# First scan of a fused state-space and two-FFN kernel: split loads, alternating PSUM tiles, new issue order

## The chip, the cores and the metric

The kernel runs on one core of a Trainium2 chip. The metric is the device time of one execution in microseconds (us); the time of a version is the median of its runs.

## What is computed

The inputs are `x` (4 batches, 8 heads, 768 steps, 32 values), a decay `a` per step, and `B`, `C` with 16 states per step. A causal scan with decay runs over the 768 steps, and two feed-forward networks follow on the 3072 rows of 256 values that it gives:

```
log_a = log(clip(a, 1e-6, 1))
per chunk:  cum = cumsum(log_a);  L = exp(cum_i - cum_j) for i >= j, else 0
            y   = ((C B^T) * L) x  +  (C state) * exp(cum)
            state = exp(sum log_a) * state + sum_j B_j x_j exp(cum_end - cum_j)
h = x @ w_in;   g = h if h > 0 else exp(h) - 1;   x2 = g @ w_out
out = ((x2 @ w1) * (x2 @ w2) @ w3) @ w_out2
```

All data are float32. Where precision matters the kernel splits a matrix into a high part, rounded to the matmul format, and a low part, the rest, and replaces one product by three matmuls (`mm3`, lines 394 to 397).

## The kernel before, in words

**Chunks and tiles.** A chunk is 128 rows of one position in the sequence (two blocks of 64 steps) for all batches and heads; there are 24 chunks of data, and four chunks make one tile of 512 rows. The first four chunks, 0 to 3, are the *first scan*. Their path is separate from that of the later ones because their L comes from the decays by TensorE, not through a store and reload in DRAM.

**One chunk of the first scan**, as steps with the letters that name them in the order string:

- `0`, `9`, `4` (`first_parts`, L430): all decays are clipped on VectorE, the first column of each block is set to zero, and the high and low parts `hl` are made.
- `A` (`at_wide`, L493): two matmuls spread the decays of the chunk over 128 partitions (8 rows by 512 columns) into a PSUM tile. I call them A0 to A3.
- `l` (`at_prep`, L504): a VectorE scan of 512 columns turns that into L, in SBUF (scan0 to scan3). It needs the constant `eye`, made in `constants`. `5` (`at_bd`, L514) is GpSimd's product of B with the last column of L.
- `U` (`first_cb`, `cb_products` L524): the products C B of a pair of chunks (CB01, CB23), 32 small matmul records a pair, from the columns `bt` and `cz` of the chunk's load. `D` (`decayed`, L539): L = CB * L on VectorE (D0 to D3).
- `J` (`first_u`): the products B x of a pair (U01, U23). `6` copies them to SBUF on ScalarE (st), `?` and `8` finish the states on GpSimd; `C` (`at_cd`, L543) decays C there, after `7` (`at_decay`, four VectorE instructions from L473).
- `Q` (`first_y`, `y_products` L595): the outputs of a pair, first the products with L (L603), then those with the states (L609), which need `?` and `C` (Y01, Y23). `z` and `Y` split them into `xTh` (ScalarE) and `xTl` (VectorE), the input of the first network.

**PSUM.** The four tiles of the first scan, `f0`, `f1`, `f2` and `acc_f`, are `[128, 2, 512]`, two banks each, and are shared: A0 and A1 go into the two halves of `f2`, A2 and A3 into `acc_f`; the CB of chunks 0 and 2 share `f0`, those of 1 and 3 share `f1`; U and the outputs of both pairs share `f2` and `acc_f`. The first three are the three buffers of the pool that later holds the products of the first network (`h`), so its first three tiles take their places.

**The first network.** `v` (`half_a`, L712) computes half a unit, 12 matmuls of 256 columns, on the outputs of chunks 0 and 1 alone; v0 and v1 are the first halves of units 0 and 1. `a` (`unit_a`, L717) is the rest (a0, a1: 12 of 256 columns; later units 12 of 512), `x r s` its gate, `b` (`unit_b`, L749) the second product. The first four `b` are plain float32 products, 8 matmul records of 512 columns. From the fifth gate on the high part is made by `h`, the low part by `i` (VectorE) or `T` (GpSimd), as `POOL_LO` says.

**Weights** come as pieces of 512 KB, loaded by SyncE's queue (SP) in the order of `PIECES` (`wi0` to `wi7`, `wo0` to `wo7` and so on), three ahead of the order string, the rest by `N`. A piece is prepared by `k` (shift; on ScalarE or VectorE by `SCALAR_LOW`), `j` (scale, ScalarE), `K` (join, VectorE), `H` (high part, ScalarE) and `I` (low part; GpSimd for `wi0`, VectorE for the others here).

**Loads of a chunk.** `at_load` (L444) loads one block of 896 columns, 448 KB, into `xbc`. The later chunks' L come by two DMAs of 128 KB each (`M`, L490), their `xbc` by `X`.

**What sets the order.** `ORDER` is a string of letters, and each letter issues the next waiting step of its kind. `in_order` (L657) chains the instructions of every engine, the DMA queues among them, in the order in which the string issues them. So an instruction that waits holds back all that stand behind it on its engine. In the kernel before, `at_first`, `constants` and the first loads stand outside `in_order`, and the framework places them.

The first steps by engine, before:

```
PE   A0 A1 A2 A3 CB01 CB23 U01 Y01 U23 Y23 v0 a0 v1 a1 a2 b0 a3 b1 CB45,U45 a4 b2 a5 Y45 b3
DVE  clip memset lo(hl) scan0 scan1 scan2 decay D0 scan3 D1 join(wi0) D2 join(wi1) xTl0 xTl0' shift(wi2) D3
SP   a, xbc0, xbc1, pr, xbc2, xbc3, wi0, wi1, wi2, store, wi3, wi4, wo0, wo1, wi5, wo2, L4, pr1, wi6, L5, xbc4, wo3, xbc5
```

Of the kernel before, what the change touches and what calls it, by code (L numbers as in the profile page):

```python
# [22 lines left out]
DM = NH * D
# [11 lines left out]


ORDER = """
094AAlAl5Al5U7UJD6lk?C6j?!DNCkKC5jD5QHN8JKzIzY66NYHk?jD8kNK?jCI8QkNvK8zzYHYNkjaIHKjvMIHkxIaPkrKaNkxsjMLrbKjXxsNrkKaRHXBj
WMIjCbsxNrLXKBWsujNkaKDHMDtbxLNjIBr?tXK?jaCskCkKNhLxiyBrCbMKzsHNjkzYWkuXHYKaIHDjNtWI?bDxXKrtPI?jsHMykIazjXYKzhYNLahiBxMT
LrbXxsrBNVuHshMbRjiCaCDtt?aDxIrVNkhKbVxijrsaSLhsTaxkjLSrb?xsrkVHsyhIbPzzYBiXCBaKNYHKhkXRuxTbrMtHtMIsbhDCNDj??kiIhKyaLjNk  # L40
zBzYHKbMIKHxYILNHarCjsIMaihCBNxkkriaXjsxXbxNrrswjLhKBaLHkIijfbNsxK1FHbrIhsNkuSSwDhijtK?bHfIjFDkaNKhtHi?BxCIyrbPzszkXKjaY
hXiTYNuxbrMDKsMbthD?kCjktaiRaxCr?swxLrLhBbHsfIHFINyazBzYTXhYKMaixrNsbxMkrLXjswBhKjikufKHLbHItF?NtCaDh?KB1IDaxTNrjsbxrsSy
SazMYkzkMYhwPjiKaHxIHCNrbIxsXrKwfshNFTufXjbktDHkFItHDahKILCwLBxTrsa?R?axCrfsbjHKIFhByHibMIzxYMrbXhszYuLaDBtt?i?wDxLafNhr
iXbFxs1NbhBCrijskyKjbkhzzY3YKu%&aSt&D3tDC&a=Th=S=xa?&?x=TNrbrsCxsbhNjirkhsyTbzKjkYKaz%&=bxh^&ira&=&=sbx=rYNhsaih3iaxNjr3
bksxrbks@jKhKa&Th=&a@=%x#rbxsrTsaS&S=&#bx=^Nh^@ia@1r#h3#^asNjxirkbK@sxrkb#@sh#jia3hKi%&b&x=31@=r#a^&sh=&ib/x=rsbh/i|ch_b
i/|m_b/GSg]e|[EncS{(1m_)|}G>3e]_g.<cn,*[(mE}G.{e],<)nE>g*{.c[,dm*(.G}.)*]e.>gn<E.,*(.{c[})m,<g,G[e,.d>nd,]c.,(m,*d}E$*e.
{G.,)*]<d.>dng$,*.E+[c{.d,md,.g$,([,d@}G@#<d]#3d@)*+e>En#^d.{(+c*@})@d#m^e.,dnG,@*g.>(]#^c[}Eme.{G@,)n<.d,<$g>]d,[(*.#cd
m,3.g}.d,E#*G{3d,^e.+)n,d]*(.>E[+*c}dm+d.<2g{e,<)n+G.,(.*d>]}c.,d[,Eme,.d{*G+nd],2*d.+E.,d*.d<)2{d>3g,*d[+c.,2(m).}G.,<g
]>e[,En,d.{c*,(m)$*}d.>g.,G*.d,]e.,d.,cn<E[d*{$(+$)m}d@,<d.>G@#e]g#.c,nE@,*[d{m(+^.G}d,e*@+d])#.*En>d.{g^#([).,^d@}c@,em
d,.g#@G,[d<nd#*](>E}<.c{em#.G,n)],*d>g+E*.d{.(,*.d}[d+c.<)m+e*.>g2nG+[<(,]d,c}Emd.{d.,G$,),e>*gn+d[<2c*.,dm(],*G.}d.,E]*  # L50
.d+.e{2g,<nE[).{d,(,d}d>),.c>$*dm,eg*.dn,G[*c.+d.<2dm+.(,$G]g$}E.d{]d,[<e,dn).+d.,E>d,c,(m+d.G,d]}${e<E.dn{(,d}<)g>).d.,
[,d>.d,dd+++++
"""
# [39 lines left out]
X_RAW = {0: "s0 0", 4: "s0 1", 2: "s1 0", 5: "s1 1", 1: "s2 0"}  # L93
P_RAW = {0: "l0 0", 4: "l0 1", 2: "l1 0", 5: "l1 1", 1: "s2 1"}, {0: "h0 0", 4: "h0 1", 2: "l2 0", 5: "l2 1", 1: "i7 1"}

XCOLS = (("x", DM), ("bn", NH * N), ("bt", 2 * R), ("cz", 2 * 2 * R), ("cp", SUB * R))
XC = sum(n for _, n in XCOLS)

@with_exitstack
def kernel(  # L100
# [358 lines left out]

# [575 lines left out]
    at_first()
    constants()
    for k in range(2):
        at_load(k)
    at_pr(0)
    for k in range(2, CPT):  # L1040
        at_load(k)
    for p in queue[:3]:
        p.load()
# [72 lines left out]
```

## Time and profile before

| | us |
|---|---|
| median of 3 runs | 520.39 (519.7 to 520.78) |
| the profiled execution, its own time | 519.32 |
| its span, first to last instruction | 517.6 |
| TensorE (PE) busy | 504.3 (97%) |
| VectorE (DVE) busy | 406.6 (79%) |
| ScalarE (ACT) busy | 338.1 (65%) |
| GpSimd (POOL) busy | 242.0 (47%) |

Busy times are sums over the span; 1.7 us of the execution's own time lie outside it. In the rows below, times are from the span's start. A timeline row has start, length, engine, line of the kernel, operation, the tile written and the tiles read, and in square brackets how long the engine sat idle before it and what ended that. Instructions of one engine overlap a little, so what a sequence costs is the distance of the starts, not the sum of the lengths.

### The profile page before, as it was taken

What the parts mean: (1) busy time and instruction counts of PE and PEld (TensorE: products, weight loads), DVE (VectorE), ACT (ScalarE), POOL (GpSimd) and SP (SyncE); (2) the same over time, 40 slices, a digit from 0 to 9 for tenths busy, and PEclk for the clock granted to TensorE, in tenths of its full rate; (3) what the DMA queues carried; (4) which work ended last, traced back from release to release, by engine and by line L of the source; (5) the groups of instructions that cost most, each with busy time, mean ns of one, the idle gap of its engine ahead of it and who ended that gap; (6) DMA issues with size and microseconds to landing.
All of it is one profiled execution on the core that took longest, in us unless ns stands there. A gap on an engine that the chain in (4) does not pass through costs nothing.

```text
span 517.6 us, 9978 instructions
## 1 busy us (share of the span) xinstructions
PE 504.3 (97%) x3978; PEld 408.4 (79%) x3978; DVE 406.6 (79%) x548; ACT 338.1 (65%) x511; POOL 242.0 (47%) x224
## 2 busy tenths in 40 slices
PE   5799999999999999999999999999999999999996
PEld 3675678788878888888788888888887888878885
DVE  5888899996657655657687669957899898988874
ACT  2786777677665666653675888766765668566631
POOL 2612252572342452641445173977487555655410
PEclk9999999999999999999999999999999999999999
DMA  8994680564360734213321223010001110001002
GB/s 293 314 286 132 214 238 20 146 180 146 123 211 5 192 125 135 80 39 95 146 82 32 91 88 128 9 63 0 1 22 41 60 43 1 1 22 41 20 1 81
DMA packets 28174, 51.04 MB, mean 99 GB/s; under 512 B 2304, under 2 KB 10880, under 8 KB 28128
## 3 DMA queue, kind: packets, MB, share of 16 engines
q1 hardware_dynamic: 27984, 50.28, 31.3%
q8 instruction: 31, 0.51, 0.4%
q10 hardware_dynamic: 144, 0.13, 0.1%
q14 instruction: 15, 0.12, 0.1%
HBM read 44.01 MB, written 6.39 MB: 97 GB/s over the span
## 4 chain that ended last, share of the span: by engine, by line
PE 95%; POOL 2%; DMA 1%; DVE 1%; SPq 0%; issue 0%; DVEq 0%; ACT 0%; POOLq 0%
PE acc L395 10%; PE acc L396 9%; PE acc L397 9%; PE h L395 9%; PE h L396 9%; PE h L397 9%; PE p L395 4%; PE p L397 4%; PE p L396 4%; PE acc L757 3%; PE p_E L395 2%; PE p_E L397 2%; PE p_E L396 2%; PE p_d L397 2%; PE p_d L396 2%; PE p_d L395 2%
## 5 line engine op out<-in xcount | busy, mean ns | idle before, releaser
L733 DVE SCALAR_TENSOR_TENSOR e<-e,h 128x1024 f32<-128x1024 f32 x44 | 53.4, 1214 | 37.3 <-ACT e L728 33.3
L726 ACT ACTIVATE e<-h 128x1024 f32<-128x1024 f32 x48 | 49.3, 1027 | 50.0 <-PE h L397 47.6
L395 PE MATMUL h<-xTh,w_in 128*128 128x512 f32 (+1 forms) x200 | 78.8, 394 | 0.4 <-DVE g L733 0.4
L396 PE MATMUL h<-xTl,w_in 128*128 128x512 f32 (+1 forms) x200 | 76.9, 384 | 0.0
L397 PE MATMUL h<-xTh,w_in 128*128 128x512 f32 (+1 forms) x200 | 76.7, 383 | 0.0
L395 PE MATMUL acc<-g,w_out 128*128 128x512 f32 x176 | 69.7, 396 | 0.0
L396 PE MATMUL acc<-g,w_out 128*128 128x512 f32 x176 | 68.6, 390 | 0.0
L397 PE MATMUL acc<-g,w_out 128*128 128x512 f32 x176 | 68.5, 389 | 0.0
L738 ACT CAST g<-e 128x1024 fp32r<-128x1024 f32 x44 | 46.1, 1050 | 17.9 <-PE acc L397 15.1
L171 DVE TENSOR_TENSOR g<-e,g 128x1024 fp32r<-128x1024 f32 x31 | 42.1, 1357 | 15.0 <-ACT g L738 14.9
L171 POOL TENSOR_TENSOR g<-e,g 128x1024 fp32r<-128x1024 f32 x13 | 32.6, 2506 | 41.5 <-ACT g L738 34.9
L728 ACT ACTIVATE e<-e 128x1024 f32<-128x1024 f32 x48 | 50.7, 1060 | 1.0
L517 POOL TENSOR_TENSOR xbc<-xbc,L 128x128 f32<-128x128 f32 x24 | 16.1, 673 | 69.0 <-DVE L L511 32.6
L395 PEld LDWEIGHTS h<-xTh,w_in 128*128 128x128 f32 x200 | 38.3, 191 | 8.4 <-DVE g L733 0.5
L397 PEld LDWEIGHTS h<-xTh,w_in 128*128 128x128 f32 x200 | 38.2, 191 | 7.3
L396 PEld LDWEIGHTS h<-xTl,w_in 128*128 128x128 f32 x200 | 38.3, 192 | 7.1 <-issue 0.5
L395 PEld LDWEIGHTS acc<-g,w_out 128*128 128x128 f32 x176 | 33.0, 188 | 7.3
L397 PEld LDWEIGHTS acc<-g,w_out 128*128 128x128 f32 x176 | 33.0, 188 | 7.0
L396 PEld LDWEIGHTS acc<-g,w_out 128*128 128x128 f32 x176 | 33.1, 188 | 6.4
L171 POOL TENSOR_TENSOR w<-raw_wc,w 128x512 fp32r<-128x512 f32 x16 | 22.5, 1410 | 25.6 <-ACT w L249 12.3
L911 POOL TENSOR_TENSOR room_l<-room_l,room_o 128x512 f32<-128x512 f32 x12 | 19.0, 1582 | 26.6 <-DVE room_o L908 18.2
L511 DVE TENSOR_TENSOR_SCAN L<-L,eye 128x512 f32<-128x512 f32 x20 | 25.8, 1298 | 0.1
(438 smaller groups left out, 1318.4 us busy)
## 6 DMA issues: line engine op xcount, KB each, us to landing
xbc<-in_xc SPq DMA_DIRECT2D x24, 448.0 KB, 6.3
raw_wc<-in_w3t SPq DMA_DIRECT2D x16, 512.0 KB, 5.9
L<-a_cut SPq DMA_DIRECT2D x40, 128.0 KB, 5.8
raw_wi<-in_w_in SPq DMA_DIRECT2D x8, 512.0 KB, 8.7
raw_wo<-in_w_out SPq DMA_DIRECT2D x8, 512.0 KB, 7.5
x_dram<-x SPq DMA_DIRECT2D x6, 512.0 KB, 4.0
room_s<-x_dram SPq DMA_DIRECT2D x12, 256.0 KB, 3.7
out_t<-out SPq DMA_DIRECT2D x11, 256.0 KB, 2.0
```

The costliest lines, as they stand in the source:

```text
L171: eng.tensor_tensor(out=lo, in0=raw, in1=hi.bitcast(F32), op=ALU.subtract)
L395: T.matmul(out, wlo, xhi, start=first, stop=False, **kw)
L396: T.matmul(out, whi, xlo, start=False, stop=False, **kw)
L397: T.matmul(out, whi, xhi, start=False, stop=last, **kw)
L511: V.tensor_tensor_scan(out=flat, data0=wide, data1=eye.rearrange("p h s -> p (h s)"), initial=0.0, op0=ALU.mult, op1=ALU.add)
L517: G.tensor_tensor(out=c["bd"], in0=c["bn"], in1=c["L"][:, :, R - 1:R].to_broadcast([P, NH, N]), op=ALU.mult)
L726: A.activation(e, h, AF.Exp)
L728: A.activation(e, e, AF.Relu, scale=-1.0, bias=1.0)
L733: V.scalar_tensor_tensor(out=gt[t, n] if plain else e, in0=e, scalar=-1.0, in1=h, op0=ALU.mult, op1=ALU.max)
L738: A.copy(hi, e)
L757: T.matmul(acc, word_of(n)[:, j, es], g[:, j], start=m == 0, stop=False)
L911: GATE[m % 2].tensor_tensor(out=s["two"], in0=s["two"], in1=s["u2"], op=ALU.mult)
```

## The change

It has four parts.

1. **Constants and decays.** The high part of `hl` is made by VectorE, not ScalarE; the copy that makes `eye` moves behind the low part of `hl`; `own` is made before the sum of `eye2`. `at_first`, `constants` and the first loads are now inside `in_order`.
2. **Loads.** The columns `bt` and `cz` stand first in a chunk's block. For chunks 0 to 3 they are loaded by a DMA of their own (192 KB, here CBn), the other 512 columns by a second one (256 KB, `rest`). `wi0` is loaded ahead of the loads of chunks 2 and 3.
3. **PSUM.** A0 and A2 go into `f2`, A1 and A3 into `acc_f`. CB, U and outputs of chunk k have columns of tile k alone (`f0`, `f1`, `f2`, `acc_f`), so the two pairs share no tile any more. Half f of a pair's outputs lies in tile f of that pair.
4. **Order.** A new `ORDER`, new choices of engine in `POOL_LO` (19 letters `T` and 25 `i`, before 13 and 31) and `SCALAR_LOW`, and `wi6`, `wi7` ahead of `wo3` in `PIECES`. No other kind of letter changes its count.

```
PE   A0 A1 A2 CB01 U01 A3 Y01 CB23 U23 v0 Y23 v1 a0 a1 a2 b0 b1 CB45,U45 a3 a4 a5 b2 Y45 a6
DVE  clip memset hi(hl) lo(hl) eye scan0 scan1 scan2 D0 D1 decay join(wi0) scan3 shift(wi2) join(wi1) D2 D3 xTl0 xTl0'
SP   a, CB0, CB1, pr, rest0, rest1, wi0, CB2, CB3, rest2, rest3, wi1, wi2, store, wi3, wi4, wo0, wo1, wi5, pr1, wo2,
     L4, L5, wi6, L6, L7, wi7, xbc4, xbc5, wo3, xbc6, xbc7
```

```diff
 ORDER = """
-094AAlAl5Al5U7UJD6lk?C6j?!DNCkKC5jD5QHN8JKzIzY66NYHk?jD8kNK?jCI8QkNvK8zzYHYNkjaIHKjvMIHkxIaPkrKaNkxsjMLrbKjXxsNrkKaRHXBj
+094AAll5AUl5kDjD7JA66?K!CN?lkC5QjNH5Uk8jKNIzDHNDz8kYJjYNKvkK66P?jI?HCKNCHIQkvzMIzkYkMYHRajNaxIMKraLjMsjxNLbrKXxsrXKbksjN
...
-POOL_LO = "001000100101000000010100101100001101000110000000"
-SCALAR_LOW = "11011000000110010000100011111001011110011100"
+POOL_LO = "011011111001101011000010101000111001000000101000"
+SCALAR_LOW = "11011001110101111001011001010001110000000101"
...
-XCOLS = (("x", DM), ("bn", NH * N), ("bt", 2 * R), ("cz", 2 * 2 * R), ("cp", SUB * R))
+XCOLS = (("bt", 2 * R), ("cz", 2 * 2 * R), ("x", DM), ("bn", NH * N), ("cp", SUB * R))
+CB = 2 * R + 2 * 2 * R
...
-        V.tensor_tensor(out=eye2[:, 0], in0=eye2[:, 0], in1=eye2[:, 1], op=ALU.add)
-        V.tensor_copy(eye, eye2[:, 0:1].to_broadcast([P, NH, R]))
...
         V.tensor_reduce(out=own, in_=head.rearrange("p (b g) -> p g b", g=2), op=ALU.add, axis=AX.X)
+        V.tensor_tensor(out=eye2[:, 0], in0=eye2[:, 0], in1=eye2[:, 1], op=ALU.add)
...
-        A.copy(hl[:, 0], t[:n])
+        V.tensor_copy(hl[:, 0], t[:n])
         yield "4"
         take_lo(V, hl[:, 1], t[:n], hl[:, 0])
+        V.tensor_copy(eye, eye2[:, 0:1].to_broadcast([P, NH, R]))
...
-        nc.sync.dma_start(all_, xc[k])
+        if k < CPT:
+            nc.sync.dma_start(all_[:, :CB], xc[k][:, :CB])
+            c["rest"] = all_[:, CB:]
+        else:
+            nc.sync.dma_start(all_, xc[k])
...
-        ck[k]["a"] = wide = first_rooms[CPT - 2 + k // 2][:, k % 2]
+        ck[k]["a"] = wide = first_rooms[CPT - 2 + k % 2][:, k // 2]
...
-        half = k // 2
-        return (first_rooms[k % 2][:, :, 4 * R * half:4 * R * half + 4 * R],
-                first_rooms[2 + half][:, :, R * (k % 2):R * (k % 2) + R])
+        return parts_of(first_rooms[k])
...
-        at = 2 * R * (1 + ks[0] // 2)
-        rooms = [by_chunk(room[:, :, at:at + 2 * R]) for room in first_rooms[2:]]
+        at = 4 * R + 2 * D
+        rooms = [by_chunk(first_rooms[k][:, :, at:at + 2 * R]) for k in ks]
...
+    def first_loads():
+        for k in range(2):
+            at_load(k)
+        at_pr(0)
+        for k in range(2):
+            at_rest(k)
+        queue[0].load()
+        for k in range(2, CPT):
+            at_load(k)
+        for k in range(2, CPT):
+            at_rest(k)
+        for p in queue[1:3]:
+            p.load()
```

## Rows read from the trace of the kernel before

**Rows 1.** Busy us by stretch: PE, PEld, DVE, ACT, POOL, granted clock, DMA

```profile
0.00:21.32 21.32, 12.55 (x297) 8.23 (x297) 15.03 (x27) 9.73 (x20) 11.02 (x29) 1.00 0.93 326
21.32:24.40 3.08, 3.08 (x18) 3.08 (x15) 2.58 (x6) 2.98 (x7) 0.79 (x3) 1.00 1.07 198
21.32:513.60 492.28, 491.72 (x3686) 400.17 (x3682) 390.82 (x520) 328.36 (x491) 230.98 (x196) 1.00 0.29 88
```

**Rows 2.** The chain that ended last, from 0 to 25 us: start, us, what

```profile
3.46 6.70 DMA xbc<-in_xc
10.20 1.13 PE f L534 x24
...
16.40 1.25 POOL w_in L171
...
20.90 0.37 PE f L609 x2
...
24.25 0.21 PE h L395
...
24.61 0.12 PE h L397
```

**Rows 3.** Timeline of PE

```profile
4.48 0.79 PE L500 MATMUL f<-a_hl,sel 8*128 8x512 f32 x1 [4.48 <-ACT a_hl L439]
...
8.47 1.56 PE L534 MATMUL f<-xbc 32*64 32x128 f32 x40
...
16.61 0.43 PE L603 MATMUL f<-L,xbc 64*32 64x64 f32 x6 [0.77 <-DVE xTl L171]
...
40.96 0.69 PE L534 MATMUL s<-xbc 32*64 32x128 f32 x32
...
42.42 0.50 PE L395 MATMUL h<-xTh,w_in 128*128 128x512 f32 x1 [0.38 <-DVE g L733]
```

**Rows 4.** Timeline of DVE

```profile
3.78 0.43 DVE L159 COPY eye<-eye 128x512 f32<-128x512 f32 x1
4.46 0.68 DVE L171 TENSOR_TENSOR a_hl<-a_f,a_hl 8x512 fp32r<-8x512 f32 x1 [0.25 <-ACT a_hl L439]
6.87 2.34 DVE L511 TENSOR_TENSOR_SCAN L<-f,eye 128x512 f32<-128x512 f32 x2 [1.73 <-PE f L500]
...
10.24 0.27 DVE L419 TENSOR_SCALAR pr<-pr 128x256 f32<-128x256 f32 x1
...
11.49 0.67 DVE L541 TENSOR_TENSOR L<-f,L 128x512 f32<-128x512 f32 x1
12.07 1.22 DVE L511 TENSOR_TENSOR_SCAN L<-acc_f,eye 128x512 f32<-128x512 f32 x1
...
16.69 0.42 DVE L171 TENSOR_TENSOR xTl<-acc_f,xTh 128x256 fp32r<-128x256 f32 x1
```

**Rows 5.** Timeline of ACT

```profile
14.66 0.66 ACT L249 CAST w_in<-raw_wi 128x512 fp32r<-128x512 f32 x1
```

**Rows 6.** Timeline of SP's queue: issues of the loads of wi2, wi5 and xbc5

```profile
5.02 1.12 SPq L212 DMA_DIRECT2D raw_wi<-in_w_in  x1
...
11.51 0.37 SPq L212 DMA_DIRECT2D raw_wi<-in_w_in  x1
...
24.46 0.34 SPq L447 DMA_DIRECT2D xbc<-in_xc  x1
```

**Rows 7.** DMA issues of the same three, KB, us from issue to landing

```profile
raw_wi<-in_w_in SPq DMA_DIRECT2D x1, 512.0 KB, 9.2
...
raw_wi<-in_w_in SPq DMA_DIRECT2D x1, 512.0 KB, 9.7
...
xbc<-in_xc SPq DMA_DIRECT2D x1, 448.0 KB, 10.2
```

**Rows 8.** Groups of the page: the gate's low part on either engine

```profile
L171 DVE TENSOR_TENSOR g<-e,g 128x1024 fp32r<-128x1024 f32 x31 | 42.1, 1357 | 15.0 <-ACT g L738 14.9
L171 POOL TENSOR_TENSOR g<-e,g 128x1024 fp32r<-128x1024 f32 x13 | 32.6, 2506 | 41.5 <-ACT g L738 34.9
```

More of the change, by code (lines that the diff above doesn't have):

```diff
@@ L37 @@
 ORDER = """
-094AAlAl5Al5U7UJD6lk?C6j?!DNCkKC5jD5QHN8JKzIzY66NYHk?jD8kNK?jCI8QkNvK8zzYHYNkjaIHKjvMIHkxIaPkrKaNkxsjMLrbKjXxsNrkKaRHXBj
-WMIjCbsxNrLXKBWsujNkaKDHMDtbxLNjIBr?tXK?jaCskCkKNhLxiyBrCbMKzsHNjkzYWkuXHYKaIHDjNtWI?bDxXKrtPI?jsHMykIazjXYKzhYNLahiBxMT
-LrbXxsrBNVuHshMbRjiCaCDtt?aDxIrVNkhKbVxijrsaSLhsTaxkjLSrb?xsrkVHsyhIbPzzYBiXCBaKNYHKhkXRuxTbrMtHtMIsbhDCNDj??kiIhKyaLjNk
-zBzYHKbMIKHxYILNHarCjsIMaihCBNxkkriaXjsxXbxNrrswjLhKBaLHkIijfbNsxK1FHbrIhsNkuSSwDhijtK?bHfIjFDkaNKhtHi?BxCIyrbPzszkXKjaY
@@ L42 @@
[L42 to L51, printed above, removed]
@@ L52 @@
-[,d>.d,dd+++++
+094AAll5AUl5kDjD7JA66?K!CN?lkC5QjNH5Uk8jKNIzDHNDz8kYJjYNKvkK66P?jI?HCKNCHIQkvzMIzkYkMYHRajNaxIMKraLjMsjxNLbrKXxsrXKbksjN
+WBKCkLXjBjCLuX8HW8aDjNktCkK?BtaxI?BDrCkNHsaxIrKVbHNKxsrjsjyKNaIzzYkPYVjKhMuxTbNDHDjtrMI?tkbs?XWkKhNVRhyXHazIzCMHTYWYKkaN
+xITrLMaxsXrBkjXLbjHKBxIkbNHsrIhsuhTLajNjVtBDCbxTKrtksaS?HKSILh1bDx?NKjkHiHIyKrbPhIsHMijIazMkYzKNRHaxIXrLBbXxYshNrTwhsLTu
+fNjbjtDkCF?DBtCbCKNBk?HjIyazMzYhKMkHYKaxNirksXaxLhXrTbjsxkIjurbNhsDKahiktL?bxBtrD?CsBSTySha1zzYPCYTuxMbrDMsXDbhtLX?CtaiB
@@ new lines @@
+?LaRxrCjsbChxiryKbMshMzwYXXafHFiHIzYbxINrBswKLjNakfHhIHiaxINFrkCjsBwxCLrNKbfsHjIFkhuhTNatK?ibxKjDHtDrbIks?NhySTSazj1YzYB
+PbxMjrMwsXKhaXHfIHFRkINaxriasxrNkswhKxTLjbfkrFBKjHLbhsBIkahiHIuxbrt?stwD?CDKfHFyKIaMiHhIMzzbYxXLrXYaisLwxhrTaNfsFBBuxbrN
+sDahktjTkjaKxKrC?tCsbx%Dr&bh=?&sT&Sy&hazzS==ibx=rYNYsuh3bt1D?Ctk?NDahijT3KykjbxK3^&r%b&s3zz&=a&Y==Y=axNrsaxhNriajshxibrk
+ksxbKjhaihKi%bx@r#b&s3&r=hsaSiS&1=@b&#h=^=xaNr@#axi@srNbjsh#xTkahKkir^bjs@^xKb@%rhsa&#T&h=&=axir=&sb/x=rsbh/i|ch_bi/|m#@
+b_3#/e|Gn3g]c[Em(^{SG3})]<e>gn_*E.(S{c[1,.)}md><|g,.G[c,*]e_mEn*g.{([,).*G}d>]e.,c<nE,m*d.{(.,).}G><g],e[cn,d.*Em,(*{G.d
+}.d],*$e<.g+nd,$).,d[>E$,*(@{d.}c.#d<m,e3@G@#d],gn#*)[E>(^+.c}dm{*e@+dn#G@^)<]g,.^d[>d.#(@*E@}d.{c.,<em#)g*,3G[>d],cn,.E
@@ new lines @@
+3m#(.,g.G{,)]}d*3>e,d*.+d[,nE*$d<.(+.c*{.d}m).+<e.+2gn>G[,d],c.(,md,G,d,*g+E}2*d.{e,dn*)+.d]<2(.>[E,*.c}.d{me,.<)n,dg>d,
+.G,[(],*c+E}2d*.{em,d.*dn<$),.d.,G>d]g,*.c+$E$,^[({@d}m)#@<d.>e@#Gg#]^d.,cn,d[*mE+@({^@d}.)#.e*+dn#d$^g.>G@,*c[#](@d<mE#
+*g{G[}d.,<)]e.>En,c.{(m,).}G>g],e,cn,*d[(m+d*.d+.E}*.d{g<e.,<Gn+d],2([*)+.E>.d,d}c,em,d{G+)],2d.>*dn<g+c[*E.2dm{(.,G}*d]
+,)e<>gn,E.*c[,d.m({.d,.),.G,g]}*d[,e*E>nd.{($+*c.,2d.m)<.d+$d,.g,$G}d]><d.de+dn,c[,d.(m.E}G,d],e$+E,g{d[<nd.,d{()}d><.),
+d.,d>.d,d+++++
@@ L55 @@
 SCALAR_Z = 4
-POOL_LO = "001000100101000000010100101100001101000110000000"
-SCALAR_LOW = "11011000000110010000100011111001011110011100"
+POOL_LO = "011011111001101011000010101000111001000000101000"
+SCALAR_LOW = "11011001110101111001011001010001110000000101"
 VECTOR_LO = 16
-PIECES = [(("w_in", "w_out")[k == "o"], "iiiiiooioioooioo"[:n].count(k)) for n, k in enumerate("iiiiiooioioooioo")] + [("wo2", m) for m in range(4)] + [("w3", m) for m in range(16)] + [
+PIECES = [(("w_in", "w_out")[k == "o"], "iiiiiooioiiooooo"[:n].count(k)) for n, k in enumerate("iiiiiooioiiooooo")] + [("wo2", m) for m in range(4)] + [("w3", m) for m in range(16)] + [
     (k, m) for m in range(4) for k in ("w2", "w1")]
@@ L456, in at_load, with at_rest @@
         c["cp"] = cols_["cp"].rearrange("p (s i) -> p s i", s=SUB)
+    def at_rest(k):
+        nc.sync.dma_start(ck[k]["rest"], xc[k][:, CB:])
     pr = {}
@@ L1034 @@
     later("0", first_parts)
[L1035 to L1043, printed above, removed]
+    in_order(at_first)
+    in_order(constants)
+    def first_loads():
[11 more added lines that the diff above has]
+            p.load()
+    in_order(first_loads)
     later("!", lambda: nc.sync.dma_start(a_cut, first_a[0]) and None)
@@ L1090 @@
         "xc": np.concatenate([
+            on_rows(B).reshape(NCHUNK, Q, 2 * R),
+            cz.reshape(NCHUNK, Q, 2 * 2 * R),
             by_chunk(x).reshape(NCHUNK, Q, DM),
             by_chunk(B).reshape(NCHUNK, Q, NH * N),
-            on_rows(B).reshape(NCHUNK, Q, 2 * R),
-            cz.reshape(NCHUNK, Q, 2 * 2 * R),
             cp.reshape(NCHUNK, Q, SUB * R),
```

## The prediction

> **What bounds the kernel now.** I read the busy time by stretch first. From 21.32 us, where v0 begins, to the last matmul at 513.6, PE is busy 491.72 of 492.28 us; before that it is busy 12.55 of 21.32 [rows 1]. So one dense stretch of PE work sets the end, and a change can gain in two ways only: that stretch begins earlier, or part of its work is done ahead of 21.32. The whole idle time within it is 0.56 us, of which 0.38 is the wait at 42.42 [rows 3]; nothing else can be won there, and stalls can be added. What follows the last matmul, four additions and a store, stays.
>
> The chain says why v0 starts at 21.32: the last load of the first four chunks lands at 10.16 (issue 3.46, 6.70 long), CB23 waits for it, then the chain runs through GpSimd, where the low part of wi0 stands among the states, to the last state products of Y23 at 20.90 [rows 2]. v0 needs only chunks 0 and 1, and their last part, xTl0', is there at 16.69 + 0.42 = 17.11 [rows 4]; the low part of wi0 is there at 16.40 + 1.25 = 17.65 [rows 2]. So v0 is held for 3.7 us by its place behind Y23.
>
> A second reading, of the waits: scan0 starts at 6.87, when A0 and A1 are both done [rows 4], though it reads A0's half only; and Y23 waits at 16.61 for xTl0, which reads other columns of the tile [rows 3]. Waits in this program are for whole tiles.
>
> [...]
>
> **Part 1, decays.** hi(hl) on DVE instead of ACT: I price it as the copy of 512 columns, 0.43 [rows 4]. Now A0 starts at 4.48 [rows 3] and lo(hl) at 4.46 [rows 4]; ahead of both stood ACT's cast from 3.81. On DVE the copy runs from about 3.70 to 4.13, so both come 0.33 earlier: lo(hl) 4.13 to 4.81. The eye copy behind it ends at 5.2, before scan0 needs it. The new place of `own` waits only for constants of GpSimd, before the decays land; cost 0. If GpSimd were late, the clip would be, one for one.
>
> **Part 2, alternating tiles.** scan0 now waits for A0 alone: its second matmul starts at 4.85 and takes 0.79 [rows 3], so scan0 starts at 5.7 instead of 6.87. Against this, A2 writes `f2`, which scan0 reads, so A2 waits until 6.9; it ends at 8.0, as scan2 wants it. A pair of scans takes 2.34 and one 1.22 [rows 4], so starts lie 1.14 apart: 5.7, 6.8, 8.0, and D0 could start at 9.1. CB01 follows A2 on PE: 40 records take 1.56 [rows 3], so its 32 take 1.2, from 7.9 to 9.1. So D0 runs at 9.1 and D1 at 9.7 (a D and the next instruction lie 0.58 apart [rows 4]); D0 is now at 11.49, because CB0 and CB2 share a tile and CB2 waits for the load of 10.16. That is 2.4 us gained on D0. U01 has a new wait: it writes the tiles that D0 and D1 read, so it goes at 9.8 and 10.4, and A3 behind it at 10.8 to 11.8.
>
> **Part 3, where that gain goes.** Behind D1 stand decay (10.24 to 11.49 is 1.25 [rows 4]) from 10.3, join(wi0) 0.6 from 11.6, scan3 from 12.2 to 13.4: scan3 is now at 12.07 [rows 4], so nothing is left of the lead. Next comes shift(wi2), and wi2 lands at 5.02 + 9.2 = 14.2 [rows 6, 7]. The bytes queued up to wi2 are the same after the change, so it lands then again, and DVE waits 0.8 us with D2 and D3 behind it. From 14.2: shift 0.4, join(wi1) 0.6, D2 0.6, D3 0.6, xTl0 0.35, xTl0' 0.42, which ends at 17.2, against 17.11 now. ACT has hi(wi0) done by 15.3 at the latest, as now (14.66 + 0.66 [rows 5]), and GpSimd its low part 1.25 later; neither is last. CB23, held by scan3 until 13.4, and U23, held by D3 until 16.4, end before 17.2.
>
> [...]
>
> **Part 4, v0 ahead of Y23.** v0 starts at 17.2, 12 matmuls at 0.21: 2.5 us, to 19.7. Y23 follows: its products with L, about 1 us, then the states, which wait for GpSimd; that chain (low part of wi0, one state update, two `own`, two decays) ends at about 20.6 by the same instructions as now, so Y23 ends near 21.3 and v1 starts where v0 starts now. Net: v0's 12 matmuls are out of the dense stretch. If the clock rises 3.1 us after v1 as it now does after v0, what is saved is 12 at the high level, 12 x 0.12 = **1.4 us**. If the rise comes by v1's start, the 3.1 us at the low level, some 14 matmuls, cost 14 x 0.09 = 1.3 less, 2.7 in all. No row shows a rise after a burst that breaks off, so I take the lower end. [...]
>
> **Part 5, the next wait.** b0 and b1 now follow a2, and CB45, U45 stand ahead of a3: after the change CB45 is reached near 36.5 (now 40.96 [rows 3], less a3's 2.75 and 1.4 to 1.8). They need xbc5. SP issues it behind four pairs of L, not two, and behind wi7, though ahead of wo3. From wi5's landing, 11.51 + 9.7 = 21.2, to xbc5's, 24.46 + 10.2 = 34.7 [rows 6, 7], 3200 KB land (wo2, wi6, wo3 512 each, two pairs of L 512, pr1 256, two xbc 896): 237 KB a us. After: 3712 KB (wo2, wi6, wi7 1536, L 1024, pr1 256, xbc 896), 15.7 us: xbc5 at 36.9. GpSimd's product and U45 follow, about 1.2 us, so a3 starts near 38.1 and a4, 2.75 later, at 40.9. a4 starts at 42.42 now [rows 3]. The lead after this point is 1.5 us. Bounds: the PE path alone gives 1.4 + 0.38 = 1.8 (the wait at 42.42 goes), or 3.1 with the early rise; below, a rate a tenth lower puts xbc5 at 38.6, and the lead is gone.
>
> **Part 6, the rest.** Six low parts go from DVE (1357 ns) to GpSimd (2506) [rows 8]: 8.1 us off DVE, 15 on GpSimd, which is idle half of the span; beside the PE stretch, cost 0, if none is late. The pieces' order and engines: 0, since each is prepared some units ahead.
>
> **Sum.** Against the profiled execution of 519.32: 519.32 - 1.5 = 517.8. The median of the runs is 1.07 above it, so I predict 520.39 - 1.5 = **518.9**.
>
> **Rivals.**
> - *The load is there and the clock rises early.* xbc5 at 36 or before, then PE sets the pace and the lead is 1.8 to 3.1: 517.3 to 518.6. For it: only a tenth more rate is needed, and the rate is a mean over a mix whose L share doubles. Against it: nothing shows an early rise. Chance 0.2.
> - *The gain is given back at CB45, or never made.* xbc5 at 38 to 38.5 leaves 0 to 0.4 us, 520.0 to 520.4; so does a wi2 that lands a us or more later, since DVE passes that on to v0. Chance 0.2.
> - *Slower: the queue of L pairs and wi7 ahead of xbc4 and xbc5.* Every us that xbc5 lands after 38.4 is a us lost, PE having nothing else in its order. At 200 KB a us it lands at 39.8 and the time is 521.8; it decides from 39.4 on, which is 204 KB a us. For it: the L loads are the smallest of the mix and come in one row. Against it: the mean of 237. Chance 0.08.
> - *GpSimd's low parts come late.* 2506 against 1357 ns on the path gate, low part, `b`; six more of them, each late by up to 1.15 us, add 0 to 7 us, 521 if two of them bite. [...] Against it: PE waits for none of the 13 now. Chance 0.06.
>
> **How the numbers follow.** Likeliest (0.46): lead 0.6 to 2.2, 518.2 to 519.8, 0.36 of it with a lead above 1.04 us, which is 0.2% and about what a measurement of this kernel can tell from no change. Faster: 0.36 + 0.2 = 0.56; same: 0.1 + 0.2 = 0.3; slower: 0.08 + 0.06 = 0.14. The range takes in all of the first two rivals and leaves out most of the last two: 517.3 to 521.0.
>
> **What would show it.** Right: scan0 at 5.7, D0 at 9.1, a DVE wait for wi2 until 14.2, v0 at 17.2 ahead of Y23, v1 near 21.3, a wait at CB45 or U45 ended by xbc5 or its product. Wrong: v1 a us or more off 21.3, the 0.12 us pace before 23 us, no wait at CB45, or idle PE between 50 and 510 us.

## The result and the profile after

The changed kernel is slower: 525.84 us (median of 4 runs, 525.08 to 526.55) against 520.05 us before, ratio 1.0121 with a 95% interval of 1.0103 to 1.0139. The prediction was 518.9 with a range up to 521.0, so it was wrong in sign. The profiled execution took 525.08 us, its span 523.0.

The first lines of the page after, engines and the gate's low part on either engine, answer to the table of before and to [rows 8]:

```profile
PE 505.6 (97%) x3978; PEld 406.8 (78%) x3978; DVE 412.7 (79%) x542; ACT 338.0 (65%) x511; POOL 255.4 (49%) x230
...
L171 POOL TENSOR_TENSOR g<-e,g 128x1024 fp32r<-128x1024 f32 x19 | 47.6, 2510 | 52.8 <-ACT g L744 52.1
L171 DVE TENSOR_TENSOR g<-e,g 128x1024 fp32r<-128x1024 f32 x25 | 35.7, 1426 | 6.5 <-ACT g L744 6.4
```

PE does the same 3978 matmuls. VectorE issues 6 instructions less (542, before 548) and is yet busy 6.1 us longer (412.7, before 406.6). That is the first sign that something in the prediction's costs is wrong.

The first scan itself went much as forecast. The timeline of DVE after (answers to [rows 4]) and that of PE (answers to [rows 3]):

```profile
5.65 1.22 DVE L519 TENSOR_TENSOR_SCAN L<-f,eye 128x512 f32<-128x512 f32 x1 [0.55 <-PE f L508]
...
9.34 1.29 DVE L549 TENSOR_TENSOR L<-f,L 128x512 f32<-128x512 f32 x2
...
12.56 1.21 DVE L519 TENSOR_TENSOR_SCAN L<-acc_f,eye 128x512 f32<-128x512 f32 x1
15.30 0.43 DVE L223 TENSOR_SCALAR raw_wi<-raw_wi 128x512 uint32<-128x512 uint32 x1 [1.53 <-DMA raw_wi<-in_w_in]
```

```profile
18.00 0.56 PE L395 MATMUL h<-xTh,w_in 128*128 128x256 f32 x1
18.36 0.41 PE L396 MATMUL h<-xTl,w_in 128*128 128x256 f32 x1
18.57 0.41 PE L397 MATMUL h<-xTh,w_in 128*128 128x256 f32 x1
...
22.57 0.39 PE L395 MATMUL h<-xTh,w_in 128*128 128x256 f32 x1
22.79 0.28 PE L396 MATMUL h<-xTl,w_in 128*128 128x256 f32 x1
22.91 0.28 PE L397 MATMUL h<-xTh,w_in 128*128 128x256 f32 x1
...
31.16 3.70 PE L763 MATMUL acc<-g,words_h 128*128 128x512 f32 x8 [1.26 <-DVE g L739]
```

scan0 stands at 5.65 (forecast 5.7), D0 at 9.34 (9.1), the wait for wi2 ends at 15.30 (14.2), v0 starts at 18.00 (17.2), v1 at 22.57 (21.3). v0's starts lie 0.21 apart, v1's 0.12: v1 already runs at the faster of the two paces that the chain of before shows [rows 2]. Counted at equal PE work (Y23 and one half unit done), the changed kernel stands at 22.57 and the one before at 24.04, so the change is 1.5 us ahead there. The row before:

```profile
24.04 0.41 PE L395 MATMUL h<-xTh,w_in 128*128 128x256 f32 x1
```

At the end it is 5.7 us behind (the last matmul starts at 518.85, before at 513.14), so some 7.2 us are lost after the part that the change is named for.

The windows and PE's waits from 27 us on show where. In the windows the columns are those of [rows 1]:

```profile
27.00:100.00 73.00, 70.20 (x720) 49.96 (x719) 67.14 (x85) 56.21 (x80) 33.08 (x33) 1.00 0.63 208
100.00:300.00 200.00, 200.00 (x1972) 165.58 (x1971) 134.20 (x179) 124.02 (x159) 89.39 (x81) 1.00 0.32 103
300.00:400.00 100.00, 97.47 (x427) 79.56 (x426) 89.03 (x98) 72.88 (x118) 64.15 (x50) 1.00 0.11 40
```

Waits of PE: line, what it waited for, us in total, times, longest:

```profile
PE acc L396 <- DVE g L171: 1.5, 2, 1.1
PE p L395 <- DVE room_l L920: 1.4, 1, 1.4
PE acc L763 <- DVE g L739: 1.3, 1, 1.3
PE p L395 <- ACT room_o L902: 0.7, 1, 0.7
PE h L395 <- DVE xTl L171: 0.4, 1, 0.4
PE p_d L396 <- DVE room_t L171: 0.2, 1, 0.2
```

PE is idle 2.8 us between 27 and 100 and 2.5 between 300 and 400, and not at all between. Five of the six lines wait for VectorE, none for GpSimd. Before, PE's whole idle time behind 21.32 us was 0.56. The six lines sum to 5.5 us. Most of the rest is that a wait here costs more than its idle time: at 397.65 a matmul starts 1.80 us after the one before it, where they otherwise lie 0.23 apart, so 1.57 for an idle time of 1.41. At 31.16, 67.70, 338.04 and 346.95 the difference is 0.16 as well; for the seven waits that makes 1.1 us, an estimate from these five.

### The profile page after: what moved, and what is told of

It reads as the page before. It is cut to its first block, busy times and chain, and to the rows that moved or that the text cites. A ratio compares the mean times of both kernels' runs of the same rounds, so it can differ in the third digit from the quotient of the medians.

```text
span 523.0 us, 9982 instructions
## 1 busy us (share of the span) xinstructions
PE 505.6 (97%) x3978; PEld 406.8 (78%) x3978; DVE 412.7 (79%) x542; ACT 338.0 (65%) x511; POOL 255.4 (49%) x230
## 4 chain that ended last, share of the span: by engine, by line
PE 71%; DVE 7%; POOL 4%; issue 2%; ACT 2%; DVEq 0%
PE acc L395 7%; PE acc L396 7%; PE acc L397 7%; PE h L395 6%; PE h L396 6%; PE h L397 6%; PE p L395 4%; PE p L396 4%; PE p L397 4%; PE p_d L396 2%; PE p_E L395 2%; PE p_E L397 2%; PE p_d L397 2%; PE p_E L396 2%; PE p_d L395 2%
## 5 line engine op out<-in xcount | busy, mean ns | idle before, releaser
L739 DVE SCALAR_TENSOR_TENSOR e<-e,h 128x1024 f32<-128x1024 f32 x44 | 53.5, 1215 | 31.1 <-ACT e L734 28.4
L171 POOL TENSOR_TENSOR g<-e,g 128x1024 fp32r<-128x1024 f32 x19 | 47.6, 2510 | 52.8 <-ACT g L744 52.1
L171 POOL TENSOR_TENSOR w<-raw_wc,w 128x512 fp32r<-128x512 f32 x16 | 25.3, 1589 | 38.1 <-ACT w L249 33.5
L397 PEld LDWEIGHTS h<-xTh,w_in 128*128 128x128 f32 x200 | 38.2, 191 | 7.3
L396 PEld LDWEIGHTS h<-xTl,w_in 128*128 128x128 f32 x200 | 38.2, 191 | 6.6
L171 DVE TENSOR_TENSOR g<-e,g 128x1024 fp32r<-128x1024 f32 x25 | 35.7, 1426 | 6.5 <-ACT g L744 6.4
L519 DVE TENSOR_TENSOR_SCAN L<-L,eye 128x512 f32<-128x512 f32 x20 | 30.8, 1546 | 0.2 <-DMA L<-a_cut 0.2
L586 POOL TENSOR_TENSOR st<-st,own 128x128 f32<-128x128 f32 (+1 forms) x24 | 15.9, 665 | 25.0 <-DVE st L579 20.5
```

What stands on the lines that cost most here:

```text
L396: T.matmul(out, whi, xlo, start=False, stop=False, **kw)
L397: T.matmul(out, whi, xhi, start=False, stop=last, **kw)
L519: V.tensor_tensor_scan(out=flat, data0=wide, data1=eye.rearrange("p h s -> p (h s)"), initial=0.0, op0=ALU.mult, op1=ALU.add)
L586: G.tensor_tensor(out=new.rearrange("p s (g d) -> p s g d", g=2), in0=new.rearrange("p s (g d) -> p s g d", g=2), in1=own.rearrange("p (o ...
L739: V.scalar_tensor_tensor(out=gt[t, n] if plain else e, in0=e, scalar=-1.0, in1=h, op0=ALU.mult, op1=ALU.max)
```

## The experiments

Two theories for the 7.2 us. **E (engines):** the new choice of engines for the gate's low parts, 19 on GpSimd instead of 13, costs, by stretching VectorE's instructions. **O (order):** the new order behind the first scan (with its pieces and its engines for shifts) leaves PE waiting on VectorE's in-order queue. A third, **W**, blames the split loads. The "six low parts" of the prediction and of the texts below are a net count: by the two `POOL_LO` strings thirteen of the 44 went to GpSimd and seven came back. So the exchange of engines tests the whole choice, not six instructions.

### The two halves of the change

`scan_alone` is the new code with the changed order up to Y23 and v1, then what is left of the order before:

```diff
 094AAll5AUl5kDjD7JA66?K!CN?lkC5QjNH5Uk8jKNIzDHNDz8kYJjYNKvkK66P?jI?HCKNCHIQkvzMIzkYkMYH
-RajNaxIMKraLjMsjxNLbrKXxsrXKbksjN
+88ajxIarKaNkxsjLrbKjXxsNrkKaRHXBj
...
-POOL_LO = "011011111001101011000010101000111001000000101000"
+POOL_LO = "001000100101000000010100101100001101000110000000"
```

with SCALAR_LOW and PIECES of before too. Expected:

> The new first scan alone: the changed code, the changed order up to Y23, v1 and the first low parts of wi0 and wi1, then the rest of the order before, with the engines and pieces of before. Two traces compared so far: the changed kernel is 1.5 us ahead at the end of a2 and 5.7 us behind at the end, so 7.2 us are lost behind the first scan. Theory E (the six low parts of the gate that went to GpSimd stretch VectorE's instructions beside them and come late) and theory O (the new order of the rest leaves less between a gate and its b) both expect that the gain of the first scan stays: 518.3 to 519.0 where before gives 520.0. Theory W (the split loads and the new places of loads make weights and decays late, which VectorE's queue passes on for good): 519.8 to 523.

Measured: **518.07 us, ratio 0.9972 (0.9960 to 0.9983)**; before gave 519.43. Its timeline of PE, and its only wait of PE from 27 us on:

```profile
16.80 0.56 PE L395 MATMUL h<-xTh,w_in 128*128 128x256 f32 x1
...
22.20 0.39 PE L395 MATMUL h<-xTh,w_in 128*128 128x256 f32 x1
22.43 0.28 PE L396 MATMUL h<-xTl,w_in 128*128 128x256 f32 x1
22.54 0.28 PE L397 MATMUL h<-xTh,w_in 128*128 128x256 f32 x1
```

```profile
PE h L395 <- DVE g L739: 0.4, 1, 0.4
```

The wait of 0.4 is the one that before has at 42.42 [rows 3]. The lead is 1.84 us at the start of v1 and 1.44 at the end. So the rebuilt first scan is worth what was forecast, 1.4 us, and everything that was lost lies in the rest of the change. W, which asked for 519.8 to 523, falls.

`rest_alone` is the complement: code, loads and order of before through Y23 and v0, then the rest of the changed order with its engines.

```diff
 ...66NYHk?jD8kNK?jCI8QkNvK8zzYHYNkjaIHKjv
-MIHkxIaPkrKaNkxsjMLrbKjXxsNrkKaRHXBj
+PMIkkMHRNaxIMKraLjMsjxNLbrKXxsrXKbksjN
```

> The other half: code and loads of before, its order through Y23 and v0, then the rest of the changed order with its engines and pieces. E and O both expect some 5 to 7 us more than before, 525 to 527. W expects 519.9 to 521.

Measured: **526.33, ratio 1.0135 (1.0115 to 1.0156)**, 6.9 us slower. Its waits are those of the changed kernel, one by one (2.0 at the first b, 1.5 for the gate's low part, 1.4 for `room_l`, 0.6, 0.5).

### Engines against order

Only the engine of each gate's low part is exchanged; every letter of the order stays.

```diff
+LO_ENG = "..."
-            take_lo(G if pool else V, lo, e, hi)
+            take_lo(G if LO_ENG[t * NA + n] == "1" else V, lo, e, hi)
```

`before_eng_after` (before, engines of the changed kernel):

> The kernel before, its order untouched letter by letter; only the engine of each gate's low part is taken from the changed kernel (19 of 44 on GpSimd, not 13). E: 2 to 7 us more, 522 to 527, VectorE's other instructions longer beside GpSimd's. O and W: no change, 519.6 to 520.6.

`after_eng_before` (the changed kernel, engines of before):

> The changed kernel, its order untouched letter by letter; only the engine of each gate's low part is that of before (13 of 44 on GpSimd). E: 518.5 to 521. O and W: 525 to 526.5, as the changed kernel. If both E and O hold a part, between.

Measured: 522.28 (ratio 1.0053, 1.0038 to 1.0067) and 524.56 (1.0101, 1.0084 to 1.0118). **Both theories hold a part.** On the order before, the new engines cost 2.85 us. Besides the 0.4 us that before has, PE waits there twice (line numbers are one higher here):

```profile
PE acc L397 <- DVE g L172: 1.0, 1, 1.0
PE s L563 <- POOL xbc L518: 0.4, 1, 0.4
```

The first is for a low part on VectorE (its 25 take 1393 ns in the mean, the 31 of before 1357 [rows 8]), the second for GpSimd itself. Taken out of the changed kernel, the new engines give back about 1.0 (1.0121 - 1.0101 of 520); the two intervals overlap, so this is not told from nothing, and other waits then take the time. The new order without them is still 6.5 us slower than `scan_alone`, measured together with it. Its five largest waits of PE from 27 us on (line numbers again one higher):

```profile
PE h L396 <- DVE xTl L172: 1.5, 1, 1.5
PE p L396 <- DVE room_l L921: 1.4, 1, 1.4
PE h L396 <- DVE e L740: 1.2, 1, 1.2
PE s L571 <- POOL xbc L526: 0.9, 1, 0.9
PE acc L764 <- DVE g L740: 0.3, 1, 0.3
```

### What low parts on GpSimd do to VectorE

On the order before, VectorE's busy time went from 406.6 (548 instructions) to 411.0 (542). By their own lengths six fewer take 6 x 1.36 = 8.1 us off it [rows 8]; it rose by 4.4, so the others became 12.5 us longer. That is 2.1 us for each of the net six, but thirteen went and seven came back, so it is not the price of one low part. One place in the trace of the changed kernel shows how. Timeline of DVE, then of POOL (its second row is the first low part and the next one together, for 64.36 to 69.56):

```profile
60.58 0.69 DVE L237 SCALAR_TENSOR_TENSOR raw_wo<-raw_wo 128x512 uint32<-128x512 uint32 x1
61.19 0.68 DVE L171 TENSOR_TENSOR w_out<-words_h,w_out 128x512 fp32r<-128x512 f32 x1
...
64.69 2.63 DVE L171 TENSOR_TENSOR w_out<-raw_wo,w_out 128x512 fp32r<-128x512 f32 x1 [0.87 <-ACT w_out L249]
67.24 0.74 DVE L171 TENSOR_TENSOR xTl<-y,xTh 128x256 fp32r<-128x256 f32 x2
67.90 2.22 DVE L237 SCALAR_TENSOR_TENSOR raw_wo<-raw_wo 128x512 uint32<-128x512 uint32 x1
```

```profile
64.36 2.40 POOL L171 TENSOR_TENSOR g<-e,g 128x1024 fp32r<-128x1024 f32 x1
...
64.36 5.20 POOL L171 TENSOR_TENSOR g<-e,g 128x1024 fp32r<-128x1024 f32 x2
```

GpSimd's two low parts end at 66.76 and 69.56. VectorE's low part of a weight, 0.68 alone, ends at 67.32, its join, 0.69 alone, at 70.12: each 0.56 us after GpSimd's. So of 0.68 us of work some 0.12 was done in the 2.07 us beside the first low part, and as little of the join beside the second: that is no slowing by a share, these two all but stood until GpSimd was done. The two `xTl` between them, which read one operand from PSUM, take 0.74 as ever, though GpSimd's second low part runs beside them. In the same trace three more joins, at 83.67, 90.75 and 93.83, took 2.58, 1.68 and 1.80 and ended 0.54 to 0.55 after GpSimd's instruction beside them.

Two more places show how far it goes. An instruction with one SBUF input stood too: in the changed kernel a shift of a weight, 0.43 alone (the row at 15.30 above), took 2.63 and ended 0.28 after a low part on GpSimd. Timeline of DVE, then of POOL:

```profile
316.39 2.63 DVE L223 TENSOR_SCALAR raw_wb<-raw_wb 128x512 uint32<-128x512 uint32 x1
```

```profile
316.20 2.54 POOL L171 TENSOR_TENSOR g<-e,g 128x1024 fp32r<-128x1024 f32 x1 [7.89 <-ACT g L744]
```

And in one place GpSimd took longer. In `after_eng_before` its product for chunk 5 took 1.33, that for chunk 4 0.48, while VectorE ran two scans with two SBUF operands (from 35.89 to 38.66):

```profile
35.77 0.48 POOL L526 TENSOR_TENSOR xbc<-xbc,L 128x128 f32<-128x128 f32 x1 [14.38 <-DMA xbc<-in_xc]
...
37.54 1.33 POOL L526 TENSOR_TENSOR xbc<-xbc,L 128x128 f32<-128x128 f32 x1
```

The dose was tried on the best version, `scan_alone`: no low part on GpSimd (`scan_vector`), and all 44 (`scan_pool`).

```diff
-POOL_LO = "001000100101000000010100101100001101000110000000"
+POOL_LO = "000000000000000000000000000000000000000000000000"
```

> The new first scan alone, with all 44 low parts of the gate on VectorE instead of 31. Theory E (a two-input instruction of GpSimd stretches those of VectorE beside it): VectorE's busy time falls although it does 13 instructions more, from some 406 to 385 to 398; the time stays, 517.6 to 518.6, or falls a little, since no PE wait hung on it. Without contention VectorE's busy time rises by 13 x 1.21 = 16 us to 422 and the time rises by 0 to 4 us.

> The new first scan alone, all 44 low parts of the gate on GpSimd instead of 13 (31 x 1.36 = 42 us off VectorE by their own lengths). Theory E: each stretches VectorE's others by some 2 us (six gave 12.5 us, thirteen taken away gave 14), so VectorE's busy time falls by no more than 10 us from 407, or rises, and PE waits for gates: 524 or more. Without contention VectorE would fall to some 365 us and the time would be 518 to 521.

Measured, with the busy us of VectorE from the pages, and of its 44 joins (L237, two SBUF inputs) and 48 gates (L739, one operand in PSUM) from the windows of those lines:

| low parts on GpSimd | time, ratio | VectorE busy (instructions) | L237 | L739 |
|---|---|---|---|---|
| 0 (`scan_vector`) | 517.87, 0.9961 (0.9947 to 0.9976) | 409.6 (562) | 32.7 | 58.2 |
| 13 (`scan_alone`) | 518.07, 0.9972 (0.9960 to 0.9983) | 407.3 (549) | 36.2 | 58.2 |
| 19 (changed kernel) | 525.84, 1.0121 (1.0103 to 1.0139) | 412.7 (542) | 42.0 | 58.3 |
| 44 (`scan_pool`) | 531.68, 1.0257 (1.0210 to 1.0304) | 402.5 (518) | 49.6 | 58.2 |

Thirty-one low parts of 1.36 us, 42 us, taken off VectorE relieve it by 4.8. The joins grow with the dose, the gates stay. The row of 19 has another order than the others; with the order of before kept, the 20 scans of the later chunks' L alone go from 25.8 (13, before) to 29.8 (19, `before_eng_after`). The new order adds to this by itself: with the engines of before VectorE is busy 412.5 us in `after_eng_before`, 5.9 more than before with the same 548 instructions. My figure for `scan_vector` was too bold: VectorE's busy time did not fall to 398 or less, it rose by 2.3 where 13 x 1.36 = 17.7 were added, so a low part on GpSimd costs VectorE's other instructions about 1.2 us on this order (15.4 / 13), and the 31 added in `scan_pool` cost as much each ((42.0 - 4.8) / 31). In `scan_pool` PE also waits for GpSimd's low parts themselves, the case that the fourth rival had priced:

```profile
PE acc L396 <- POOL g L171: 6.0, 2, 4.1
```

```profile
345.00:350.00 5.00, 4.32 (x13) 3.39 (x14) 1.17 (x1) 0.00 (x0) 4.92 (x4) 0.69 0.00 0
```

The second fence is the window around the longest: behind a wait of 4.1 us, which ends at 345.7, the granted clock (the column behind the engines') is 0.69 of full speed in this window, and its 13 matmuls keep PE busy for 4.32 us, 0.33 each, where 155 matmuls take 34.96 from 365 to 400, 0.23 each, at a granted clock of 1.00. So this wait was paid for again after it. PE is busy 510.0 us in all, 5.6 more than in `scan_alone`; how much of that is the clock was not separated.

### Where the order costs

`order_head` is the changed order up to chunks 10 and 11 (about 100 us) and the order before behind it; `order_tail` the complement. Engines of the low parts as before.

```diff
-order: changed, to the end
+order: changed, to CB10,11; from there the steps left, as before puts them
```

> The changed order up to the products C B and B x of chunks 10 and 11 (about 100 us), the rest in the order of before; the engine of every gate's low part as before. So far the new order alone, with the engines of before, costs 6.5 us over the new first scan alone (524.56 against 518.07). Theory O1 (the order costs where VectorE's queue is nearly full, between 27 and 100 us): 4 us or more over the first scan alone, 522 to 523, and no idle PE behind 110 us. Theory O2 (the loss is made late, in the second network): 518.5 to 519.5.

> The complement: new first scan, the order of before up to the same products of chunks 10 and 11, then the changed order; engines and pieces of before. O1: 1.5 to 2 us over the first scan alone, 519.6 to 520.2, with the wait near 397 us of 1.4 us as the only large one. O2: 522 or more.

Measured: 526.80 (1.0136, 1.0117 to 1.0155) and 530.60 (1.0201, 1.0169 to 1.0233). `order_head` missed both its numbers, and `order_tail` lies in the range of O2 for another reason, because the seam between the two orders makes waits of its own: one of 8.3 us at 111.8 in `order_tail`, four of 0.6 to 1.1 between 116 and 145 in `order_head`. What can be read is where nothing is lost: behind 145 us `order_head` has no idle PE, and behind the seam `order_tail` has the 1.4 us wait for `room_l` and two of 0.2. The price of each half by itself stays open by these two runs.

So the places were moved one by one. `due_first` is `after_eng_before` with six steps moved:

```diff
-DVE  ... decay1 lo(wi4) join(wo0) scan4 gate(a0) ...
+DVE  ... lo(wi4) join(wo0) gate(a0) decay1 scan4 ...
-DVE  ... lo(wo5) lo(gate a5) xTl6 xTl6' ...
+DVE  ... xTl6 xTl6' lo(wo5) lo(gate a5) ...
-DVE  ... join(w3 piece 0) gate(tile 1, unit 3) ...
+DVE  ... gate(tile 1, unit 3) join(w3 piece 0) ...
-SP   ... wi7 xbc4 xbc5 ...
+SP   ... xbc4 xbc5 wi7 ...
```

> The changed kernel with the engines of before for the gate's low parts (524.56 us) and six steps of its order moved, nothing else: the decays of tile 1 and the scan of chunk 4 behind the gate of a0; the low part of wo5 and that of the gate of a5 behind the two xTl of chunks 6 and 7; the join of one w3 piece behind the gate of tile 1's fourth unit; the load of wi7 behind those of chunks 4 and 5. In the trace these stand in VectorE's (and SP's) queue ahead of what PE waits for at 29.95 us (0.3), 38.92 (0.9), 68.78 (1.5) and 97.68 (1.2). Theory Q (the place in the in-order queue is the cause): these waits go and 3 to 4.5 us with them, 520.0 to 521.5. Theory F (VectorE has too much work before 100 us in any order): the waits come back a few us later, 523 or more.

`due_first_eng_after` has the same moves with the changed kernel's own engines:

> The same six moves in the changed kernel with its own engines (19 low parts on GpSimd; 525.84 us). Q: the waits at 31.16 (1.3 us) and 67.70 (0.4) go; the one at 93.96 (1.1), for a low part on VectorE that stands behind instructions stretched to 1.7 to 2.6 us beside GpSimd, and the later ones stay: 523.5 to 524.8. F: 525.3 or more. The difference to the run with the engines of before is then the engines' price, 2 to 4 us.

Measured: **521.66 (1.0044, 1.0026 to 1.0062)** and 525.51 (1.0121, 1.0089 to 1.0152). Waits of PE in `due_first`, and the place of the second in its timeline of DVE:

```profile
PE acc L763 <- DVE g L739: 1.7, 1, 1.7
PE p L395 <- DVE room_l L920: 1.4, 1, 1.4
PE p_d L396 <- DVE room_t L171: 0.2, 1, 0.2
```

```profile
389.46 1.77 DVE L171 TENSOR_TENSOR room_o<-room_s,room_o 128x512 fp32r<-128x512 f32 x1
391.16 1.77 DVE L171 TENSOR_TENSOR room_h<-room_l,room_h 128x512 fp32r<-128x512 f32 x1
392.85 0.67 DVE L920 TENSOR_TENSOR room_l<-room_l,p 128x512 f32<-128x512 f32 x1
```

In `due_first` all four waits named are gone and 2.9 us with them, a little less than Q's 3 to 4.5; 1.7 came back at b1, where my move had put decay1 and two scans ahead of the next gate. With 19 low parts on GpSimd the same moves bring nothing that can be measured (525.51 against 525.84), as theory F had it for these engines: the wait at b1 is 1.8 there, that for a low part at 93.8 stays at 1.2, and those at 337 and 346 stay. At this order the choice of engines costs 3.85 us (525.51 - 521.66). The last fence shows what holds the remaining large wait: PE wants the tile `p` that L920 reads, and L920 stands behind two low parts of 0.68 us that both take 1.77 beside GpSimd.

`due_first_2` moves three places more:

```diff
-DVE  ... gate(a0) decay1 scan4 scan5 join(wo1) gate(a1) ...
+DVE  ... gate(a0) decay1 join(wo1) gate(a1) scan4 scan5 ...
-DVE  ... lo(room_o) lo(room_h) product L920 ...
+DVE  ... lo(room_o) product L920 lo(room_h) ...
```

> As the run with six steps moved (521.66 us), with three places more in VectorE's queue: the scans of chunks 4 and 5 behind the gate of a1, not ahead of it (there PE waits 1.73 us at 34.65), and one gate product of the second network ahead of a low part that it stands behind (there PE waits 1.41 us at 393.58, in every run with the changed order of the second network). Engines of the gate's low parts as before. Theory Q: both waits go, 3 us with them: 518.2 to 519.2, as the new first scan alone with the order of before (518.07); nine places in the queues would then be the whole price of the new order. Theory F: the waits come back elsewhere, 520.5 or more.

Measured: **519.53 (0.9995, 0.9985 to 1.0004)**, 5.0 us under `after_eng_before` and 0.3 above the range of theory Q. Waits of PE left:

```profile
PE h L395 <- DVE st L579: 0.8, 1, 0.8
PE p L395 <- DVE room_l L911: 0.4, 1, 0.4
PE p_d L396 <- DVE room_t L171: 0.2, 1, 0.2
```

Nine places in the queues are 5.0 of the 6.5 us (5.5 of 6.7 by the ratios to before, as these runs were not measured together). `due_first_2` keeps the changed kernel's pieces and shift engines, so what these cost is within the 1.5 left to `scan_alone`. Waits for VectorE are in it as well, 1.4 us against 0.4 in `scan_alone`; what would move them was not tried.

### The split loads

`scan_unsplit` is `scan_alone` with each chunk's load in one DMA again.

```diff
-        if k < CPT:
-            nc.sync.dma_start(all_[:, :CB], xc[k][:, :CB])
-            c["rest"] = all_[:, CB:]
-        else:
-            nc.sync.dma_start(all_, xc[k])
+        nc.sync.dma_start(all_, xc[k])
```

> The new first scan alone, each chunk's load in one DMA of 448 KB again (C B columns still first in it, wi0 still ahead of chunks 2 and 3). By the steps of the prediction the split costs the queue next to nothing and serves CB01 only: 518.1 to 519.0, CB01 up to 0.5 us later. By theory W (a fixed price of each DMA in the queue) four DMAs less bring wi0 and wi2 1 us or more earlier and the time down to 517.0 to 517.5.

Measured: 518.28 (0.9970, 0.9960 to 0.9981), the same as with the split; W's 517.0 to 517.5 falls. CB01 starts at 7.99 and D0 at 9.25 (with the split 8.06 and 9.33): not the C B columns but A2 and the scans set them, so the split neither helps nor costs.

## Why the prediction was wrong

- **Parts 1 and 2** held: scan0, D0 and D1 within 0.25 us. The split loads, priced at nothing, turned out to bring nothing either.
- **Part 3**: wi2's landing, forecast as 14.2, was 15.3 in the profile after and 13.9 in `scan_alone`, with the same loads ahead of it: off by 1.1 and by 0.3 us, and the term had no spread.
- **Part 4**: that the 1.4 us came out is luck, for two terms of the sum were off and cancelled. Y23 ended near 22.2 in `scan_alone` (22.6 in the changed kernel), not 21.3: it did not wait for GpSimd, as the sum had it, but stood right behind a v0 that had itself waited 0.45 us for a join. Against that, the faster pace had come before v1, so v1's 12 matmuls went at 0.12. In the changed kernel the lengths of Y23's matmuls fall from 0.44 to 0.22 at 21.4. That is the early rise of the first rival, which I had called shown by nothing. The sum's 0.21, 0.12 and 3.1 us are those of the trace of before, where matmuls of 256 columns start 0.21 apart up to 24.26 and 0.12 from 24.45 on, 3.1 us after 21.32; that a clock makes the difference was my reading, and no run shows it: the granted clock reads 1.00 there [rows 1] and from 0 to 27 us of the changed kernel. What failed is the step from "no row shows a rise after a burst that breaks off" to the lower end: these runs show one.
- **Part 5** named the right wait, not its whole cause. In `after_eng_before` PE waits 0.9 us at U45 for GpSimd's product, and its lead at a4 is 0.3 us (42.09 against 42.42 [rows 3]), as the second rival had it; but the product took 1.33 instead of 0.48, which is most of that wait. In the changed kernel GpSimd waits for xbc5 until 38.2 (forecast 36.9): wi5 landed at 23.9, not 21.2, though what followed came at 260 KB a us, not 237. PE does not show that wait, since b0's wait of 1.26 has made CB45 late already (38.2).
- **Part 6 is the step that failed**: "beside the PE stretch, cost 0, if none is late" and "the pieces' order and engines: 0". In their place the runs show 2.85 us for the engines on the order before (about 1.0, not told from nothing, in the changed kernel, and 3.85 on the order of `due_first`) and 6.5 us for the order. The first was priced by the instructions' own lengths [rows 8], and for six moves where thirteen went and seven came back; what they do to the neighbours on VectorE was left out, though VectorE is busy 79% of the span, and 64 of the 73 us between 27 and 100 (67 after). The second was not priced at all: the new string has some 1600 letters behind the first scan, and the prediction followed only those as far as a6.
- The fourth rival had the right culprit, at 0.06, and its price reached 7 us; but its mechanism, PE waiting for GpSimd's low part, appears only with all 44 there. In the changed kernel PE waits for VectorE, which is late beside GpSimd (the wait at 93.96 is for a low part that stands behind joins of 2.58, 1.10 and 1.68 us).
- The third rival, xbc5 late behind wi7 and the L pairs, cost at most the 0.9 us at U45.

The sum, as far as measured together: before 519.43; first scan -1.4 (518.07); new order +6.5 (524.56). The engines' 1.0 on top comes from the ratios and is not told from nothing; on the other two orders it is 2.85 and 3.85.

## What to carry to other kernels

Price a step that moves to GpSimd by what it does to VectorE as well: count VectorE's instructions on SBUF that run beside it, those with two inputs above all, two of which here took 2.63 and 2.22 us for 0.68 and 0.69 of work. Where a new order comes with a change, the part that the change is named for can be right and small and the rest decide; test it by joining the new beginning to the old remainder, which here gave the best version, 518.07 (517.87 with no low part on GpSimd, not to be told apart). In a queue in fixed order that is nine tenths full (VectorE from 27 to 100 us of the changed kernel: 67 of 73), what PE waits for next goes ahead of what is due later; one low part or scan too early was a wait of 0.4 to 1.7 us here.

## What the runs showed of the hardware that I had not expected

- In the changed kernel two VectorE instructions with two SBUF operands each ended 0.56 us after the low part on GpSimd beside them (0.68 became 2.63 at 64.69, 0.69 became 2.22 at 67.90), and a shift with one SBUF operand ended 0.28 after one (0.43 became 2.63 at 316.39); 48 gates with one operand in PSUM took 58.2 to 58.3 us with 0, 13, 19 and 44 low parts on GpSimd.
- With that, moving 42 us of work from VectorE to GpSimd lowered VectorE's busy time by only 4.8 us (407.3 in `scan_alone`, 402.5 in `scan_pool`).
- In `scan_alone` and in the changed kernel v1's starts lie 0.12 us apart, though Y23's small matmuls stand between it and v0, whose starts in the changed kernel lie 0.21 apart; in `scan_pool`, after a wait of 4.1 us deep in the dense stretch, the granted clock was 0.69 in the window of 5 us around its end.
